# First pair's queries and keys read in fp32 by SyncE's queue and converted on chip, with the opening's order redone around it

One core of one Trainium2 chip. The metric is the device time of one execution in microseconds (us), the median of several.

## The reference

Attention with a bucketed relative-position bias, then a bilinear feed-forward layer on its output.

```python
scores = (q @ k.T) / sqrt(64) + bias_table[bucket]     # q, k, v: (8, 8, 576, 64) fp32
attn   = softmax(scores)                               # normalised after the product with v
x      = (attn @ v) -> (4608, 512)
out    = ((x @ w_a) * (x @ w_b)) @ w_out               # w_a, w_b: (512, 1536), w_out: (1536, 512)
```

## The kernel before

All work is bf16 in the matmuls. The bias enters as a product: the kernel exponentiates the bias table, writes it to DRAM as a padded table (`bias_tab`), and reads it back shifted per partition into `W`; VectorE multiplies the exponentials by `W`. Heads go in pairs (32 pairs; pairs 0 to 3 are the first batch). The first 8 pairs, "the opening", run from a hand-made list of tokens; each engine and each queue takes its own instructions in the order of the list.

```python
    def load4(src, dst, b, h0, h1):                  # GpSimd's queue: fp32 in DRAM, bf16 in SBUF
        nc.gpsimd.dma_start(out=dst[:, 256 * h0:256 * h1]..., in_=src[b, h0:h1, 0:SM, :]...)
    # ...
    nc.sync.dma_start(out=bt_sb[0:NB, :], in_=bias_table)
    nc.scalar.dma_start(out=bl_sb[0:NB, :], in_=bass.AP(...))       # last row, broadcast
    nc.sync.dma_start(out=oh_sb[0:NB, :], in_=oh_handle.ap())
    nc.scalar.dma_start(out=ident[:, :], in_=id_handle.ap())
    # ... VectorE: bt_sb - bl_sb; ScalarE: exp; TensorE: table by one-hot; VectorE: copy out
    nc.sync.dma_start(out=tab.ap(), in_=tab_sb[0:H, :])             # the table's write
    def load_w(hp, y0, y1):                                         # <W, <R: bias loads
        nc.gpsimd.dma_start(out=W_sb[hp][:, :, y0:y1], in_=bass.AP(tensor=tab, ...))
    # ...
    trb = ps_tr.tile([128, 1024], BF16, tag="tr", name="trb")       # one PSUM tile, two halves
    def tr_half(): ...                                              # in turn
```

Tokens: `<k0` a load; `TK`/`TQ`/`TZ`/`X` transposes of keys, queries, tail rows, results; `CK`/`CQ`/`CZ`/`CX` the copy out of PSUM, with `:A` for ScalarE and `:D` for VectorE; `S` scores, `E` exponential, `M` product with `W`; `T`, `ET`, `MT` the same for the tail; `AV` product with the values, `N` its normalisation; `FA`, `HA`, `FB`, `G` one bilinear unit; `w2` two filler matmuls on zeros; `P..` zero pads.

The softmax here doesn't subtract the row's maximum and nothing guards it: scores larger than these inputs give would overflow.

Of the kernel before, what the change touches and what calls it, by code (L numbers as in the profile page):

```python
# [13 lines left out]
def kernel(  # L14
# [11 lines left out]
    nc = tc.nc  # L26
    FP32 = mybir.dt.float32
    BF16 = mybir.dt.bfloat16
# [4 lines left out]
    NB = 32  # L33
    NM = 4
    SM = 128 * NM
# [3 lines left out]
    NT = B * S  # L39
# [21 lines left out]
    NR = 256  # L61
# [9 lines left out]
    assert bucket[0] == NB - 1  # L71
    oh_np = np.zeros((NB, NR), dtype=np.float32)
    oh_np[bucket, np.arange(NR)] = 1.0
    oh_handle = nc.inline_tensor(oh_np.astype(ml_dtypes.bfloat16), name="oh_const")
    id_handle = nc.inline_tensor(np.eye(128).astype(ml_dtypes.bfloat16), name="id_const")

    oh_sb = const.tile([128, NR], BF16, name="oh_sb")
    ident = const.tile([128, 128], BF16, name="ident")
    bt_sb = const.tile([128, H], FP32, name="bt_sb")
    bl_sb = const.tile([128, H], FP32, name="bl_sb")  # L80
    eb_sb = const.tile([128, H], BF16, name="eb_sb")
# [30 lines left out]
    tab_sb = wo_sb[:, :, :].rearrange("p a b -> p (a b)")[:, 0:TB]  # L112
    xn_sb = [wpool.tile([128, NT], BF16, name=f"xn{mc}") for mc in range(NMC)]
    ob_last = wpool.tile([128, DM], FP32, name="ob_last")
    g_sb = [wpool.tile([128, DM], BF16, name=f"g{df}") for df in range(NDF)]


# [99 lines left out]
    def pad_x(i, eng):  # L217
        pad(eng, XG[i][64:128, 4, :, :], 64, 128)


    nc.sync.dma_start(out=bt_sb[0:NB, :], in_=bias_table)
    nc.scalar.dma_start(out=bl_sb[0:NB, :],
                        in_=bass.AP(tensor=bias_table.tensor, offset=(NB - 1) * H,
                                    ap=[[0, NB], [1, H]]))
    nc.sync.dma_start(out=oh_sb[0:NB, :], in_=oh_handle.ap())
    nc.scalar.dma_start(out=ident[:, :], in_=id_handle.ap())
    nc.vector.memset(zero_sb[:, :], 0.0)
    nc.vector.memset(tab_sb.bitcast(FP32)[0:H, :], TWO_ONES)
    pad_ones(0)
# [79 lines left out]
    def copy(eng, out, in_):  # L309
        if eng is nc.scalar:  # L310
            nc.scalar.activation(out=out, in_=in_, func=ACTF.Copy)
        else:
            nc.vector.tensor_copy(out=out, in_=in_)
# [298 lines left out]
    def copy_x(p, jqs, eng):  # L612
        b, hp = divmod(p, 4)
        c0 = SM * B + ST * b
        ps = st[p]["tx", jqs[0]]
        q0, q1 = 128 * jqs[0], min(SM, 128 * jqs[-1] + 128)
        copy(eng, xn_sb[hp][:, SM * b + q0:SM * b + q1], ps[:, 0:q1 - q0])
        if jqs[-1] == 4:
            copy(eng, xn_sb[hp][:, c0:c0 + ST], ps[:, SM - q0:S - q0])
# [98 lines left out]
    def v_next(s):  # L718
# [7 lines left out]
    ACT = nc.scalar  # L726

    opening = """
        <k0 <q0 <k1 <q123h0 <k23 <tk <W0 <v0 <W1 <vtb <vta <tq <W2 <R0 <v1 <Wta <q123h1 <W3 <Wtb <R1
        <wa0 <k4 <wb0 <R2 <R3 <q4 <k5 <uq <q7 <q5 <wa1 <wb1 <k6 <uk <vt1b <k7 <vb1a <vb1b <vt1a <wa2 <q6  # L730
        <wb2 <wo TK0 PC0:A TQ0 PF1:D PX1:D PV1:A PU0:D CK0:A CQ00:D w1 S001 PX0:D CQ01:A S000 E001 E000
        w1 TQ30 PC1:D TK1 CK1:D TQ10 CQ10:D S011 E011 CQ30:D TK3 S100 E100 TZ1 CK3:D S301 M001 TQ20
        PV0:D TK2 E301 S101 E101 CQ20:D CK2:D w1 S200 E200 CZ1:D M000 w1 KS w1 S201 EK w2 S010 E201 V0:D
        M101 TZ0 M100 M200 M201 AV00 N00 CZ0:A AV10 E010 X00 CX00:A S300 E300 N10 T0 V1:D X10 CX10:A
        M010 ET0 AV20 TQ11 TQ21 M011 N20 CQ11:A S110 S111 CQ21:A E110 X20 M301 TQ31 M300 AV30 T1 PW:D
        MT0 AV01 CX20:D M110 E111 N30 ET1 X30 M111 CQ31:A T2 ET2 S210 CX30:D E210 PF0:A LH FA0a N01 HA0a
        MT1 TK4 X01 T3 AV11 ET3 CX01:D S211 PU1:D FB0a FA1a E211 CK4:D HA1a N11 X11 G0a M210 S310 MT2
        CX11:A E310 FB1a G1a S311 FA2a HA2a TQ4 M211 CQ4:A FB2a AV21 E311 FA3a HA3a TQ5 MT3 M310 S43 S42
        CQ5:A G2a FB3a N21 M311 TK5 E43 E42 TZ0x G3a CZ0x:D AV31 LV CK5:D N31 FA4a HA4a X21 TQ7 CQ7:A
        S41 E41 S52 E52 CX21:D FB4a FA5a HA5a X31 G4a TK6 M43 FB5a CX31:D S40 E40 S53 G5a FA0b FB0b  # L740
        CK6:D M41 TZ1x HA0b G0b CZ1x:D S51 FA1b FB1b E53 M53 HA1b G1b E51 TK7 CK7:D M40 FA2b HA2b S50
        E50 FB2b FA3b G2b HA3b V2:D T4 FB3b FA4b V3:D ET4 G3b S70 E70 M42 MT4 M52 HA4b FB4b G4b TQ6 T5
        ET5 M50 CQ6:A AV40 N40 MT5 M51 FA5b S71 E71 HA5b S73 FB5b AV41 G5b M70 N41 S72 E73 FA6f E72 T6
        M73 M71 HA6f FB6f G6f AV50 N50 S62 ET6 MT6 E62 S61 FA7f HA7f M62 AV51 N51 TH S60 E61 M61 FB7f
        G7f E60 M60 S63 E63 M63 FA8f HA8f M72 T7 FB8f G8f AV60 N60 ET7 MT7 FA9f HA9f FB9f G9f AV70 FA10f
        FB10f N70 HA10f G10f AV71 FA11f N71 FB11f X71 HA11f G11f AV61 N61 X70 FO00 FO01 FO02 HO0 CX70:D
        CX71:D
    """

    h0 = (0, 1)  # L750
# [2 lines left out]
    def step(token):  # L753
# [34 lines left out]
        if kind == "TQ":  # L788
            tr_qh(p, i[1]) if len(i) > 1 else tr_q(p)
        elif kind == "CQ":  # L790
            copy_qh(p, i[1], eng) if len(i) > 1 else copy_q(p, eng)
        elif kind == "TK":
            tr_k(p)
        elif kind == "CK":
            copy_k(p, eng)
        elif kind == "TZ":
            tr_tails(second, p)
        elif kind == "CZ":
            copy_tails(second, p, eng)
        elif kind == "KS":  # L800
            tail_keys0()
        elif kind == "EK":
            ex_keys0()
        elif kind == "S":
            qk_half(p, i[1], (i[2],)) if first else qk(p, 0, (i[1],))
        elif kind == "E":
            ex_half(p, i[1], i[2]) if first else ex(p, i[1])
        elif kind == "M":
            mul_half(p, i[1], i[2]) if first else mul(p, i[1])
        elif kind == "T":  # L810
            qk_tail(p)
        elif kind == "ET":
            ex_tail(p)
        elif kind == "MT":
            mul_tail(p)
        elif kind == "V":
            b, g = divmod(p, 2)
            v_in(b, 4 * g, 4 * g + 4, eng)
        elif kind == "AV":
            av_mm(p, jqs, *((ps_ff, "ffn") if first and i[1] == 0 and p % 2 else ()))  # L820
        elif kind == "N":
            av_norm(p, jqs)
            if 4 <= p < 7 and i[1] == 1:
                t_x(p)
        elif kind == "X":
            tr_x(p, jqs)
        elif kind == "CX":
            copy_x(p, jqs, eng)
        elif kind == "PV":
            pad_vt(0, p, eng)  # L830
        elif kind == "PC":
            pad_vt(1, p, eng)
        elif kind == "PU":
            pad_blocks(ZB[1], p, eng)
        elif kind == "PF":
            pad_blocks(tl[0], p, eng)
        elif kind == "PX":
            pad_x(p, eng)
        elif kind == "PW":
            copy(eng, Wt_sb[:, :, 0:64], Wt_sb[:, :, 64:128])  # L840
        elif kind == "LH":
            load_half(2, 0)
            load_half(2, 1)
        elif kind == "TH":
            t_half(2, 0)
        elif kind == "LV":
            load_vt(2)
        else:
            raise ValueError(token)
# [83 lines left out]
```

## Time and profile before

| | us |
|---|---|
| median of the first three runs | 414.23 (414.06 to 414.74) |
| profiled span | 412.2 |
| first scores / first exponential | 7.37 / 8.01 |
| first bias load issued / first product with it | 8.31 / 11.69 |
| first bilinear matmul | 26.55 |

The prediction shows the lines that carry its reading. One more view matters for what follows: what GpSimd's queue, on which nearly all loads are issued, waits for. In the order of time (start, length, engine, line, output and input; in brackets the idle time before it and what ended it):

```profile
8.31 0.72 POOL L252 DMA_DIRECT2D W<-bias_tab  x1 [2.66 <-DMA bias_tab<-wo]
...
28.97 0.76 POOL L270 DMA_DIRECT2D wa<-in_moe_w_a_dram  x1 [1.95 <-DMA wb<-in_moe_w_b_dram]
```

The first is the wait for the table's write. The second is a wait for the first part of `w_b`, issued at 19.39. Its landing, by the trace, was at 28.68 us (GpSimd's next issue follows 0.29 later); the first unit that reads it started at 29.43. So about 0.75 us is all the room a faster start has at that point.

### The profile page before, as it was taken

The page shows a single profiled execution, that of the slowest core. Times are in us where ns is not written, and L with a number is a line of the kernel's source. Part 1 is how long each engine was busy: PE and PEld are TensorE (multiplying, and loading weights), DVE is VectorE, ACT ScalarE, POOL GpSimd, SP SyncE. Part 2 cuts the span into 40 slices and gives each one's busy share as a digit, 9 for nine tenths or more (in the row PEclk, how much of TensorE's full clock was granted, in tenths as well). Part 3 has the DMA queues.
Part 4 walks back from the last instruction along what each step waited for, and adds up shares of the span by engine and source line. Part 5 has one row for each costly group of instructions (what it writes and reads, how often), then busy time and mean ns, then how long its engine had stood idle before and what let it go on. Part 6 is the DMA issues. An engine that isn't in the chain of part 4 may idle for free.

```text
span 412.2 us, 8768 instructions
## 1 busy us (share of the span) xinstructions
PE 404.5 (98%) x3473; PEld 210.0 (51%) x3473; DVE 240.8 (58%) x568; ACT 251.3 (61%) x384; POOL 133.6 (32%) x191
## 2 busy tenths in 40 slices
PE   8999999999999999999999999999999999999996
PEld 3576656455555455455444555555545554444443
DVE  3898997366745665476656764667547652421320
ACT  4998992676748665677556765767486642322321
POOL 6967547788029300960079004300000000000000
PEclk9999999999999999999999999999999999999999
DMA  8999999999979914995299709960520012002004
GB/s 104 179 202 189 206 166 144 160 193 142 87 133 159 139 34 91 155 129 90 41 161 143 116 16 126 127 92 17 117 67 16 17 40 78 0 9 95 2 2 102
DMA packets 135786, 42.05 MB, mean 102 GB/s; under 512 B 113688, under 2 KB 130968, under 8 KB 135744
## 3 DMA queue, kind: packets, MB, share of 16 engines
q0 software_dynamic: 81712, 20.27, 56.3%
q1 hardware_dynamic: 48592, 11.87, 18.6%
q10 hardware_dynamic: 5440, 9.34, 7.2%
q8 instruction: 27, 0.44, 0.5%
q14 instruction: 15, 0.12, 0.1%
HBM read 39.18 MB, written 9.45 MB: 118 GB/s over the span
## 4 chain that ended last, share of the span: by engine, by line
PE 94%; DVE 2%; ACT 2%; DMA 1%; issue 1%; ACTq 0%; POOL 0%; POOLq 0%
PE pb L633 23%; PE pa L633 23%; PE po L670 22%; PE av L569 8%; PE qk L406 7%; PE av L559 2%; PE av L563 2%; PE qkh L446 1%; PE qkt L479 1%; DMA qn<-in_q_dram 1%; PE trb L321 1%; ACT ath L452 1%; PE trb L415 1%; PE trb L609 0%; DVE ath L461 0%
## 5 line engine op out<-in xcount | busy, mean ns | idle before, releaser
L430 ACT ACTIVATE at<-qk 128x1024 bf16<-128x1024 f32 x112 | 113.3, 1028 | 27.5 <-DMA out_dram<-ob 10.3
L643 DVE TENSOR_TENSOR g<-pb,ha 128x512 bf16<-128x512 f32 (+1 forms) x114 | 75.6, 664 | 75.0 <-PE pb L633 58.9
L633 PE MATMUL pb<-xn,wb 128*128 128x512 bf16 (+1 forms) x456 | 112.1, 368 | 0.2 <-DVE g L643 0.2
L633 PE MATMUL pa<-xn,wa 128*128 128x512 bf16 (+1 forms) x456 | 112.1, 368 | 0.0
L640 ACT ACTIVATE ha<-pa 128x512 f32<-128x512 f32 (+1 forms) x114 | 66.2, 581 | 67.7 <-PE pa L633 66.2
L670 PE MATMUL po<-wo,g 128*128 128x512 bf16 x420 | 98.2, 379 | 0.0
L435 DVE TENSOR_TENSOR at<-at,W 128x1024 bf16<-128x1024 bf16 x112 | 75.1, 686 | 22.2 <-ACT at L430 22.1
L633 PEld LDWEIGHTS <-wa 128*128 128x128 bf16 x456 | 41.2, 98 | 46.3 <-issue 6.6
L633 PEld LDWEIGHTS <-wb 128*128 128x128 bf16 x456 | 40.6, 97 | 43.6 <-issue 5.2
L670 PEld LDWEIGHTS <-g 128*128 128x128 bf16 x420 | 38.9, 98 | 44.9 <-issue 2.5
L675 ACT ACTIVATE ob<-po 128x512 f32<-128x512 f32 x34 | 20.4, 600 | 39.9 <-PE po L670 33.6
L569 PE MATMUL av<-vm,at 128*128 128x65 bf16 x896 | 41.2, 193 | 0.0
L569 PEld LDWEIGHTS <-at 128*128 128x128 bf16 x896 | 37.4, 97 | 6.3
L132 POOL DMA_DIRECT2D qn<-in_q_dram x48 | 36.4, 807 | 12.0 <-PE qk L406 6.9
L170 POOL DMA_DIRECT2D vt<-in_v_dram x12 | 7.4, 620 | 98.9 <-PE av L563 98.1
L580 DVE RECIPROCAL rc<-av 128x6 f32<-128x6 f32 (+1 forms) x64 | 11.9, 186 | 45.2 <-PE av L569 40.8
L141 POOL DMA_DIRECT2D kn<-in_k_dram x48 | 36.2, 794 | 1.4 <-issue 0.7
L559 PE MATMUL av<-vt,att 128*128 128x130 bf16 x152 | 33.6, 221 | 0.0
L406 PE MATMUL qk<-QB,KB 64*128 64x512 bf16 x192 | 29.1, 381 | 0.0
L582 DVE TENSOR_TENSOR XG<-av,rc 128x384 bf16<-128x384 f32 (+2 forms) x64 | 27.2, 425 | 2.2
L506 ACT ACTIVATE att<-qkt 128x640 bf16<-128x640 f32 x24 | 16.8, 701 | 13.0 <-PE qkt L480 13.0
L559 PEld LDWEIGHTS <-att 128*128 128x128 bf16 x152 | 15.0, 98 | 6.5
(104 smaller groups left out, 327.0 us busy)
## 6 DMA issues: line engine op xcount, KB each, us to landing
out_dram<-ob ACTq DMA_DIRECT2D x31, 256.0 KB, 3.1
vn<-in_v_dram POOLq DMA_DIRECT2D x16, 256.0 KB, 5.8
kn<-in_k_dram POOLq DMA_DIRECT2D x48, 64.0 KB, 5.0
qn<-in_q_dram POOLq DMA_DIRECT2D x48, 64.0 KB, 4.4
wa<-in_moe_w_a_dram POOLq DMA_DIRECT2D x3, 512.0 KB, 7.4
wb<-in_moe_w_b_dram POOLq DMA_DIRECT2D x3, 512.0 KB, 9.2
wo<-in_moe_w_out_dram POOLq DMA_DIRECT2D x1, 1536.0 KB, 15.6
xn<-XG SPq DMA_TRANSPOSE x52, 3.0
```

Source lines behind the costliest of these rows:

```text
L132: nc.gpsimd.dma_start(out=by_tile(qn[b % 2])[:, h0 // 4, t, :, :], in_=q[b, h0:h1, 128 * t:128 * t + 128, :].transpose([1, 0, 2]))
L141: nc.gpsimd.dma_start(out=by_tile(kn[b % 2])[:, h0 // 4, t, :, :], in_=k[b, h0:h1, t:SM:NM, :].transpose([1, 0, 2]))
L406: nc.tensor.matmul(out=ps[:, hh, :], lhsT=kT[r, t, :], rhs=qT[r, :, :], start=True, stop=True)
L430: nc.scalar.activation(out=at[:, :, :], in_=ps[:, :, :], func=ACTF.Exp, scale=scale)
L435: nc.vector.tensor_tensor(out=at[:, :, :], in0=at[:, :, :], in1=w[:, :, S - 1 + t:S - 1 + t - SM:-1], op=MULT)
L559: nc.tensor.matmul(out=pav[:, slot, :, :], lhsT=weights_tail(p, jq), rhs=vt[i][:, :, hp, :], start=True, stop=True)
L569: nc.tensor.matmul(out=pav[:, slot, hh, :], lhsT=weights(p, t, hh, jq), rhs=vm[i][:, 2 * hp + hh, t, :], start=False, stop=True, skip_grou ...
L582: nc.vector.tensor_tensor(out=xg[:, jqs[0]:jqs[0] + m, :, :], in0=pav[:, 0:m, :, 0:Dh], in1=rc[:, 0:m, :].unsqueeze(3).to_broadcast([128, ...
L633: nc.tensor.matmul(out=ps[:, 0:n], lhsT=w[df // 4][:, mc, 128 * (df % 4):128 * (df % 4) + 128], rhs=xn_sb[mc][:, 512 * c + lo:512 * c + lo ...
L640: nc.scalar.activation(out=ha[:, 0:n], in_=ff["pa", df, lo][:, 0:n], func=ACTF.Copy)
L643: nc.vector.tensor_tensor(out=g_sb[df][:, lo:lo + n], in0=ff["pb", df, lo][:, 0:n], in1=ff["ha", df, lo][:, 0:n], op=MULT)
L670: nc.tensor.matmul(out=po[:, :], lhsT=g_sb[df][:, 128 * tt:128 * tt + 128], rhs=wo_sb[:, df, :], start=(df == 0), stop=(df == NDF - 1))
```

## The change

The intent: GpSimd's queue delivered the first pair's keys at 4.37 us (transposed from 4.70) and its queries at 6.15. SyncE's queue issues sooner (its first two loads at 0.74 and 1.21 us, GpSimd's at 1.25 and 2.06). The change leaves the casting to GpSimd's queue, which did it before; whether SyncE's could cast, no run here tries. So the two are read in fp32 into columns of `xn` that are still unused, and converted by ScalarE and VectorE. The two constants become one load, both bias inputs go to ScalarE's queue, and the whole list is ordered anew.

```diff
-    nc.sync.dma_start(out=bt_sb[0:NB, :], in_=bias_table)
+    kq32 = [xn_sb[i][:, NT - 1024:NT].bitcast(FP32) for i in range(2)]
+    def load_first(x, dst):
+        nc.sync.dma_start(out=dst.rearrange("p (h x) -> p h x", x=256),
+                          in_=x[0, 0:2, 0:SM, :].rearrange("h (p t) d -> p h (t d)", t=NM))
+    nc.sync.dma_start(out=cn_sb[:, :], in_=cn_handle.ap())       # one-hot and identity together
+    load_first(q, kq32[1])
+    load_first(k, kq32[0])
+    nc.scalar.dma_start(out=bt_sb[0:NB, :], in_=bias_table)
     nc.scalar.dma_start(out=bl_sb[0:NB, :], ...)
-    nc.sync.dma_start(out=oh_sb[0:NB, :], in_=oh_handle.ap())
-    nc.scalar.dma_start(out=ident[:, :], in_=id_handle.ap())
@@ the list: loads @@
-        <k0 <q0 <k1 <q123h0 <k23 <tk <W0 <v0 <W1 <vtb <vta <tq <W2 <R0 <v1 <Wta <q123h1 <W3 <Wtb <R1
+        <k1 <q123h0 <k23 <tk <tq <W0 <W1 <v0 <vtb <vta <W2 <q123h1 <W3 <R0 <v1 <Wta <Wtb <R1 <wa0 <k4
@@ the list: start @@
-        TK0 PC0:A TQ0 PF1:D PX1:D PV1:A PU0:D CK0:A CQ00:D w1 S001 PX0:D CQ01:A S000 E001 E000
+        PX0:A PU1:A YK0:D YQ0:A TQ0 CQ00:D CQ01:A TK0 CK0:D PU0:A PC1:D w1 S001 S000 PC0:D PV1:D E001
 [the rest of the list, all in a new order, is cut]
+        elif kind == "YK":
+            copy(eng, kn[0][:, 0:512], kq32[0])
+        elif kind == "YQ":
+            copy(eng, qn[0][:, 0:512], kq32[1])
```

More of the change, by code (lines that the diff above doesn't have):

```diff
@@ L73 @@
     oh_np[bucket, np.arange(NR)] = 1.0
-    oh_handle = nc.inline_tensor(oh_np.astype(ml_dtypes.bfloat16), name="oh_const")
-    id_handle = nc.inline_tensor(np.eye(128).astype(ml_dtypes.bfloat16), name="id_const")
-    oh_sb = const.tile([128, NR], BF16, name="oh_sb")
-    ident = const.tile([128, 128], BF16, name="ident")
+    cn_np = np.zeros((128, NR + 128), dtype=np.float32)
+    cn_np[0:NB, 0:NR] = oh_np
+    cn_np[:, NR:] = np.eye(128)
+    cn_handle = nc.inline_tensor(cn_np.astype(ml_dtypes.bfloat16), name="cn_const")
+    cn_sb = const.tile([128, NR + 128], BF16, name="cn_sb")
+    oh_sb = cn_sb[:, 0:NR]
+    ident = cn_sb[:, NR:NR + 128]
     bt_sb = const.tile([128, H], FP32, name="bt_sb")
@@ L728 @@
     opening = """
-        <k0 <q0 <k1 <q123h0 <k23 <tk <W0 <v0 <W1 <vtb <vta <tq <W2 <R0 <v1 <Wta <q123h1 <W3 <Wtb <R1
-        <wa0 <k4 <wb0 <R2 <R3 <q4 <k5 <uq <q7 <q5 <wa1 <wb1 <k6 <uk <vt1b <k7 <vb1a <vb1b <vt1a <wa2 <q6
-        <wb2 <wo TK0 PC0:A TQ0 PF1:D PX1:D PV1:A PU0:D CK0:A CQ00:D w1 S001 PX0:D CQ01:A S000 E001 E000
-        w1 TQ30 PC1:D TK1 CK1:D TQ10 CQ10:D S011 E011 CQ30:D TK3 S100 E100 TZ1 CK3:D S301 M001 TQ20
-        PV0:D TK2 E301 S101 E101 CQ20:D CK2:D w1 S200 E200 CZ1:D M000 w1 KS w1 S201 EK w2 S010 E201 V0:D
@@ L734 @@
-        M101 TZ0 M100 M200 M201 AV00 N00 CZ0:A AV10 E010 X00 CX00:A S300 E300 N10 T0 V1:D X10 CX10:A
-        M010 ET0 AV20 TQ11 TQ21 M011 N20 CQ11:A S110 S111 CQ21:A E110 X20 M301 TQ31 M300 AV30 T1 PW:D
-        MT0 AV01 CX20:D M110 E111 N30 ET1 X30 M111 CQ31:A T2 ET2 S210 CX30:D E210 PF0:A LH FA0a N01 HA0a
-        MT1 TK4 X01 T3 AV11 ET3 CX01:D S211 PU1:D FB0a FA1a E211 CK4:D HA1a N11 X11 G0a M210 S310 MT2
-        CX11:A E310 FB1a G1a S311 FA2a HA2a TQ4 M211 CQ4:A FB2a AV21 E311 FA3a HA3a TQ5 MT3 M310 S43 S42
@@ L739 @@
-        CQ5:A G2a FB3a N21 M311 TK5 E43 E42 TZ0x G3a CZ0x:D AV31 LV CK5:D N31 FA4a HA4a X21 TQ7 CQ7:A
-        S41 E41 S52 E52 CX21:D FB4a FA5a HA5a X31 G4a TK6 M43 FB5a CX31:D S40 E40 S53 G5a FA0b FB0b
-        CK6:D M41 TZ1x HA0b G0b CZ1x:D S51 FA1b FB1b E53 M53 HA1b G1b E51 TK7 CK7:D M40 FA2b HA2b S50
-        E50 FB2b FA3b G2b HA3b V2:D T4 FB3b FA4b V3:D ET4 G3b S70 E70 M42 MT4 M52 HA4b FB4b G4b TQ6 T5
-        ET5 M50 CQ6:A AV40 N40 MT5 M51 FA5b S71 E71 HA5b S73 FB5b AV41 G5b M70 N41 S72 E73 FA6f E72 T6
@@ L744 @@
-        M73 M71 HA6f FB6f G6f AV50 N50 S62 ET6 MT6 E62 S61 FA7f HA7f M62 AV51 N51 TH S60 E61 M61 FB7f
-        G7f E60 M60 S63 E63 M63 FA8f HA8f M72 T7 FB8f G8f AV60 N60 ET7 MT7 FA9f HA9f FB9f G9f AV70 FA10f
-        FB10f N70 HA10f G10f AV71 FA11f N71 FB11f X71 HA11f G11f AV61 N61 X70 FO00 FO01 FO02 HO0 CX70:D
-        CX71:D
+        <k1 <q123h0 <k23 <tk <tq <W0 <W1 <v0 <vtb <vta <W2 <q123h1 <W3 <R0 <v1 <Wta <Wtb <R1 <wa0 <k4
+        <wb0 <R2 <q4 <q5 <R3 <uq <k5 <wa1 <q7 <wb1 <uk <vt1b <vb1a <k7 <q6 <wa2 <vt1a <k6 <wb2 <vb1b <wo
@@ new lines @@
+        PX0:A PU1:A YK0:D YQ0:A TQ0 CQ00:D CQ01:A TK0 CK0:D PU0:A PC1:D w1 S001 S000 PC0:D PV1:D E001
+        E000 TK1 PV0:A CK1:D TQ10 TQ20 CQ10:D S011 E011 w1 TQ30 CQ30:D PF1:D S101 CQ20:D E101 TK2 w2 TZ1
+        CK2:D S200 M001 S100 CZ1:D E200 M000 E100 TK3 w2 KS CK3:D EK M101 TZ0 S201 E201 CZ0:D V0:D w2
+        S300 E300 M100 M201 M200 w2 S301 E301 AV10 TQ21 CQ21:A N10 PX1:D S010 E010 M300 M301 M010 T0
+        TQ11 CQ11:A ET0 AV00 T1 X10 ET1 TQ31 CX10:A N00 V1:D CQ31:A M011 PW:D MT0 S110 E110 AV30 N30 X00
@@ new lines @@
+        AV20 N20 S111 CX00:A MT1 T2 X30 E111 M111 X20 AV01 S210 CX20:A CX30:A M110 FA0a TK4 ET2 N01 T3
+        AV11 N11 E210 CK4:A HA0a X01 S211 MT2 ET3 FB0a FA1a E211 HA1a G0a X11 CX01:A S310 CX11:D E310
+        M211 S311 FB1a FA2a G1a M210 PF0:D LH M310 TQ5 TQ4 MT3 FB2a HA2a G2a CQ5:A FA3a CQ4:A AV21 N21
+        E311 M311 TZ0x TK5 FB3a S42 HA3a CK5:D CZ0x:A S43 E42 FA4a G3a HA4a AV31 LV TQ7 N31 X21 CX21:D
+        E43 S41 FB4a G4a FA5a CQ7:A X31 CX31:D S52 E41 M42 HA5a FB5a G5a FA0b TZ1x M41 E52 S40 S53 FB0b
@@ new lines @@
+        CZ1x:D HA0b G0b E40 FA1b E53 M40 V2:D TK7 FB1b S51 HA1b G1b CK7:D S50 E51 M52 FA2b HA2b FB2b G2b
+        M53 T4 FA3b M43 TK6 FB3b E50 S70 HA3b FA4b G3b CK6:D ET4 MT4 M51 E70 HA4b FB4b M50 TQ6 T5 ET5
+        G4b CQ6:A AV40 FA5b N40 S71 E71 V3:D S73 HA5b MT5 FB5b AV41 N41 E73 G5b M71 S72 E72 M72 FA6f M73
+        T6 FB6f AV50 HA6f G6f S62 ET6 E62 S61 N50 MT6 M62 FA7f HA7f AV51 N51 TH E61 M61 S60 FB7f G7f E60
+        M60 S63 E63 M63 FA8f M70 T7 FB8f HA8f G8f ET7 AV60 N60 FA9f HA9f MT7 FB9f G9f AV70 N70 FA10f
@@ L748 @@
+        FB10f AV71 HA10f FA11f G10f FB11f HA11f N71 X71 AV61 G11f N61 X70 FO00 FO01 FO02 CX71:D HO0
+        CX70:D
     """
```

## The prediction

> **What bounds the kernel now.** I read the page's first two parts, then the core view, then busy time by stretch, then the chain that ended last, then the opening instruction by instruction. Part 1 and part 2 of the page:
>
> ```profile
> PE 404.5 (98%) x3473; PEld 210.0 (51%) x3473; DVE 240.8 (58%) x568; ACT 251.3 (61%) x384; POOL 133.6 (32%) x191
> ...
> PE   8999999999999999999999999999999999999996
> ```
>
> TensorE is busy for 404.5 of 412.2 us. What any change of order can win is therefore small: 412.2 - 404.5 = 7.7 us, plus the filler matmuls on zeros that only keep the array busy. The busy-time view by stretch (busy us of each engine, then granted clock, DMA share and GB/s) says where that is:
>
> ```profile
> 0.00:5.00 5.00, 3.81 (x14) 1.09 (x16) 2.77 (x15) 2.22 (x4) 3.95 (x10) 1.00 0.54 69
> 5.00:8.00 3.00, 2.14 (x25) 1.14 (x19) 0.89 (x4) 0.98 (x2) 0.65 (x1) 1.00 1.14 143
> 8.00:14.00 6.00, 6.00 (x74) 3.17 (x70) 3.42 (x9) 4.91 (x6) 5.69 (x9) 1.00 1.20 147
> 14.00:24.00 10.00, 8.58 (x142) 5.71 (x142) 9.36 (x22) 9.66 (x15) 9.84 (x14) 1.00 1.12 182
> 24.00:60.00 36.00, 35.98 (x466) 23.92 (x463) 33.24 (x95) 32.80 (x51) 19.47 (x28) 1.00 1.45 196
> ```
>
> From 24 us to 60 us TensorE has 0.02 us to spare, and filler is absent there. From 14 to 24 us VectorE (9.36 of 10) and ScalarE (9.66 of 10) are the tight ones and TensorE has 1.42 us idle plus 1.65 us of filler (the same view for the filler's tile alone). Before 8 us all wait for data. So the opening is a start-up delay, then some 10 us paced by exponentials and table products, and then 388 us of matmuls that the change doesn't touch. The chain that ended last, in order of time (start, length, what), shows what the start-up waits for:
>
> ```profile
> 0.63 0.62 issue
> 1.25 0.81 POOL kn L123
> 2.06 4.09 DMA qn<-in_q_dram
> 6.16 0.04 issue
> 6.20 0.64 PE trb L321 x8
> 6.83 0.54 PE warm L237
> 7.37 1.02 PE qkh L446 x8
> ```
>
> The first queries are the second transfer on GpSimd's queue; they land 4.09 us after their issue, the query transposes start at 6.20 and the first scores at 7.37. The timeline has the first key transposes at 4.70, the first exponential at 8.01, and an idle ScalarE for 0.84 us before the third one at 10.79. That 6.20 is what the change attacks.
>
> [...] small loads of SyncE and ScalarE landed 1.7 to 1.9 us after their issue began, a 256 KB store of ScalarE's queue took 3.1, the first key load of GpSimd 3.45 (1.25 to 4.70). [...] the 128x512 copy in the trace took 598. [...] there are two rates, though its granted clock reads 1.00 throughout: a filler matmul lasts 0.61 us at 8.33 and 0.39 us at 13.88, four 256-column score matmuls 0.61 at 13.35 and 0.39 at 14.21. So everything TensorE does before about 13.5 us is slow, on the chain[...].
>
> **The change, part by part.**
> Removed: two casting loads at the head of GpSimd's queue, 0.82 + 0.74 = 1.56 us of its time. The next pair's keys and the other queries move up to 1.25 and 2.06, so they should land about 1.5 us sooner. The bias-table loads that follow do not gain: GpSimd idles 2.7 us for the table's write until 8.31 as it is.
> Added on SyncE's queue: one constant load (96 KB, replaces two), then queries and keys in fp32, 256 KB each. Issues there take 0.41 us, so they start at about 0.74, 1.2 and 1.6. With 1.9 us for a small load, and 1.2 more for 256 KB (3.1 - 1.9), I put the queries at 1.2 + 3.0 = 4.2 and the keys, sharing engines with GpSimd's loads, at about 4.8 (estimates).
> Added work: one ScalarE copy of 128x512 (0.60 us) and one VectorE copy (0.42 us for the 128x512 copy in the trace). ScalarE is idle enough there: its exponential of the table ends near 3.4 and the two small pads put behind it near 4.1. Queries ready at 4.2 + 0.6 = 4.8, keys at 4.8 + 0.4 = 5.2.
> Path: query transposes 4.9 to 5.5 and key transposes 5.5 to 6.1 (0.57 us each at the slow rate, now back to back), key copy on VectorE with latency to about 6.6, first scores about 6.6. Before: 7.37. Gain 0.8 us. The first exponential moves from 8.01 to about 7.2. With the next pair's data early, the 0.84 us hole before the third exponential should close: 0.8 more for ScalarE.
> Moved against it: both table inputs are now on ScalarE's queue, so the second is issued at about 1.2, not 0.74. The table exponential was held by the 1.28 us function-table load until 2.97; the input now arrives at about 3.0, plus 0.15 for the subtraction. So table write and first bias load come some 0.3 us later (8.31 to 8.6). The first table product on VectorE (11.69) can't start before that load lands: it moves to about 12.0.
> VectorE then loses 0.3 at the start, but the key and query copies that lay between its first products are already done: 0.42 + 0.42 for two copies and 0.28 for a pad before the second product at 14.40. I expect it 0.5 to 1 us ahead by 20 us. ScalarE could be 1.6 us ahead. AV products need both, so the lesser counts: 0.5 to 1 us by 24 us. Re-ordering may recover some of the 1.42 us of TensorE idle between 14 and 24: I allow 0.4. From 24 us on TensorE is full and the lead is carried to the end. Three more filler matmuls (10 for 7 in the list) cost 0.2 to 0.4 each only if they land where real work waits; I charge 0.2.
> Sum: -0.8 (middle of the lead) - 0.4 + 0.2 = -1.0, and 414.23 - 1.0 = 413.2. [...]
>
> **The rivals.**
> 1. The bias table takes over as the bound. The start-up gain is real but VectorE's products wait for the table loads, which are later by 0.3. For it: GpSimd's 2.7 us wait for the table write, and VectorE at 9.36 of 10 us. Against: VectorE had 2.58 us idle between 8 and 14 which the new order can fill with copies. Then 414.2 to 414.6.
> 2. The fp32 loads are slow: 512 KB plus 96 KB in one queue beside GpSimd's reads; the keys land at 6 instead of 4.8, and since VectorE's conversion is ahead of the query copy in its strict order, everything waits for them. For it: the median landing of GpSimd loads under load is 4 to 7 us. Against: engines are only 0.72 of 2 us busy from 2 to 4 us. First scores then at 7.8, and the time 414.3 to 415.
> 3. The whole 1.5 us lead of the early loads goes through, with an earlier end of the slow rate and the holes at 18 to 23 us closed. For it: TensorE's chain is made of slow-rate work from 6.2 to 13.4, about 7 us that would take 40% less at the fast rate. Against: ScalarE then has no room, being full from 10.8. Then 411 to 412.
>
> **Range and chances.** The three runs before spread over 0.7 us, so noise is below the effect's size. The middle case is 413.1; rivals 1 and 2 reach 415, rival 3 reaches 411. Eight times in ten between 411.5 and 414.8. Faster by over 2% would need 8.3 us, more than all idle TensorE time of 7.7 us: nearly excluded. Slower by over 2% would need the new list to open holes of 8 us; the list keeps the same work, and the order from 24 us on is nearly the same: 1%.
>
> **What would show it right or wrong.** In the changed profile: query transposes near 4.9, first scores near 6.6, first exponential near 7.2, no hole of 0.8 us between the second and third exponential, first table product near 12.0, first bilinear matmul 0.5 to 1 us before 26.55, TensorE full from there. Wrong if the transposes still start after 6; if VectorE waits for the bias load beyond 12.5; or if the first bilinear matmul gains and the end does not, which would mean a wait after 26 us that I did not see.

The sum came to 413.2. The term that took it from there to the middle case of 413.1, a shade of 0.1 us for an earlier end of the slow rate, was not shown, nor is the earlier end that rival 3 supposes. Two estimates come from the trace without saying so: a filler matmul's 0.2 to 0.4 us (spacing 0.22 us in the two at 16.31, 0.43 in the five at 1.19) and the 40% of rival 3 (eight transposes 0.57 us in the chain at 9.28, 0.34 at 27.16). GpSimd's first key load, which it puts at 3.45 us by the start of the transposes, landed in 3.1 by the trace.

## The result

416.69 us (416.59 to 417.42, six runs), the kernel before in the same rounds 414.43 (413.61 to 415.46). The ratio is 1.0058, 95% interval 1.0042 to 1.0074: 2.4 us slower, outside the predicted range of 411.5 to 414.8 and of the opposite sign. Ratios here and below are the mean time of one kernel's fast runs over that of the other's of the same rounds, so not quite the ratio of the medians quoted. A control later (e11, the same kernel once more) gave 1.0065.

The page of the changed kernel, its engine and slice lines:

```profile
PE 402.5 (97%) x3424; PEld 210.7 (51%) x3476; DVE 240.5 (58%) x566; ACT 251.6 (61%) x388; POOL 132.5 (32%) x189
...
PE   7989999999999999999999999999999999999996
```

Busy time by stretch of the changed kernel, the same columns as in the prediction:

```profile
0.00:5.00 5.00, 3.30 (x8) 0.79 (x8) 2.23 (x12) 2.48 (x5) 3.86 (x9) 1.00 0.60 140
5.00:8.00 3.00, 2.63 (x24) 1.28 (x25) 1.55 (x5) 0.94 (x3) 0.00 (x0) 1.00 1.32 174
8.00:14.00 6.00, 5.53 (x68) 2.87 (x65) 3.62 (x10) 4.20 (x6) 3.95 (x6) 1.00 0.68 84
14.00:24.00 10.00, 8.85 (x138) 5.67 (x137) 9.39 (x23) 9.98 (x14) 9.74 (x15) 1.00 1.16 185
24.00:60.00 36.00, 33.64 (x451) 23.53 (x449) 29.02 (x84) 30.00 (x51) 18.45 (x26) 1.00 1.44 196
```

Three rows differ from before. Up to 5 us the DMA engines move 140 GB/s in place of 69: the first pair now comes as fp32, and the next loads start earlier. From 8 to 14 us they move 84 GB/s in place of 147, and GpSimd issues for 3.95 us in place of 5.69. From 24 to 60 us VectorE falls from 33.24 to 29.02, ScalarE from 32.80 to 30.00 and TensorE from 35.98 to 33.64. Some matmul records are missing in this trace (3,424 matmuls for 3,476 weight loads), so TensorE's figure is too low; the control's trace, in which none are missing, has 29.75, 30.69 and 34.53. Less work got done in these 36 us. The clock column reads 1.00 everywhere; the trace has no clock record before 14.88 us here (13.86 before), and the slower rate ahead of it shows only in the length of the matmuls (two fillers 1.03 us at 12.14, 0.60 at 14.85).

Instruction by instruction, first the two lines of the kernel before that count here, then the start of the changed kernel:

```profile
8.01 1.94 ACT L452 ACTIVATE ath<-qkh 128x1024 bf16<-128x1024 f32 x2 [0.28 <-PE qkh L446]
11.69 0.69 DVE L461 TENSOR_TENSOR ath<-ath,W 128x1024 bf16<-128x1024 bf16 x1
```

```profile
4.63 0.63 ACT L320 ACTIVATE qn<-xn 128x512 bf16<-128x512 f32 x1
5.31 0.64 PE L330 MATMUL trb<-cn_sb,qn 128*64 128x128 bf16 x8
5.83 0.43 DVE L322 CAST kn<-xn 128x512 bf16<-128x512 f32 x1 [0.98 <-DMA xn<-in_k_dram]
...
7.50 1.03 PE L455 MATMUL qkh<-QT,KT 64*128 64x256 bf16 x8
...
8.14 1.94 ACT L461 ACTIVATE ath<-qkh 128x1024 bf16<-128x1024 f32 x2 [0.84 <-PE qkh L455]
...
13.14 0.69 DVE L470 TENSOR_TENSOR ath<-ath,W 128x1024 bf16<-128x1024 bf16 x1 [0.44 <-DMA W<-bias_tab]
```

The first exponential is not 0.8 us earlier but 0.13 later, and the first table product 1.45 later. The chain that ended last says why the table is late:

```profile
1.19 2.28 DMA bl_sb<-in_bias_table_dram
...
4.87 4.90 DMA bias_tab<-wo
9.77 0.28 issue
10.05 0.88 POOL W L261 x2
...
20.10 8.41 DMA kn<-in_k_dram
28.51 0.04 issue
28.55 0.41 PE trb L330 x8
```

The second bias input lands at 3.47; the table's write is issued 0.58 us later than before (4.87 against 4.29) and takes 4.9 us to land in place of 3.7 (4.29 to 8.03), so the first bias load is issued at 10.05 in place of 8.31. In this trace GpSimd's queue carries that delay to later loads, down to the keys of pair 4, for which TensorE waits until 28.55.

One trace of a start says only so much, though. The control e11 is the same kernel and lost as much time. In its trace the second input landed at 3.00, the write was issued at 4.40 and the first product ran at 12.62; the first bias load came at 9.18:

```profile
9.18 1.45 POOL L261 DMA_DIRECT2D W<-bias_tab  x2 [4.28 <-DMA bias_tab<-wo]
```

That is 0.87 us later than before, not 1.74, and TensorE waits for no keys there. Of the eleven traces with these loads and the second input second on ScalarE's queue, seven issue the write at 4.39 to 4.47 and four at 4.86 to 5.06. So the slow write shows in both traces of the changed kernel (4.9 and 4.5 us to land), the late input and the wait for keys in one only, and the loss is there without these two. What TensorE waited for from 14 to 60 us (total, times, longest), changed kernel:

```profile
PE trb L330 <- DMA kn<-in_k_dram: 0.8, 1, 0.8
PE av L578 <- DVE vm L322: 0.7, 1, 0.7
PE qkt L494 <- ACT att L523: 0.5, 1, 0.5
PE qk L415 <- ACT at L439: 0.4, 1, 0.4
PE trb L618 <- ACT QT L320: 0.3, 1, 0.3
PE warm L246 <- issue: 0.2, 1, 0.2
```

and in the kernel before:

```profile
PE qkh L446 <- ACT QT L311: 0.6, 1, 0.6
PE trb L609 <- DVE XG L582: 0.5, 1, 0.5
```

From this I took two theories. T: the bias table's path is the new bound. L: the new list costs by itself. More came later.

### The profile page after: what moved, and what is told of

It is laid out like the page before. It is cut to its first block, busy times and chain, and to the rows that moved or that the text cites. A ratio compares the mean times of both kernels' runs of the same rounds, so it can differ in the third digit from the quotient of the medians.

```text
span 415.3 us, 8728 instructions
## 1 busy us (share of the span) xinstructions
PE 402.5 (97%) x3424; PEld 210.7 (51%) x3476; DVE 240.5 (58%) x566; ACT 251.6 (61%) x388; POOL 132.5 (32%) x189
## 4 chain that ended last, share of the span: by engine, by line
PE 87%; DMA 4%; POOL 2%; ACT 2%; issue 2%; DVE 2%; ACTq 0%; DVEq 0%
PE pb L642 22%; PE pa L642 22%; PE po L679 22%; PE qk L415 7%; PE av L578 7%; PE av L568 2%; DMA kn<-in_k_dram 2%; PE av L572 2%; PE qkt L488 1%; DMA bias_tab<-wo 1%; POOL W L261 1%; PE trb L424 1%; DMA bl_sb<-in_bias_table_dram 1%; ACT att L523 0%; DVE ath L470 0%
## 5 line engine op out<-in xcount | busy, mean ns | idle before, releaser
L642 PE MATMUL pa<-xn,wa 128*128 128x512 bf16 (+1 forms) x439 | 110.6, 368 | 0.7
L679 PE MATMUL po<-wo,g 128*128 128x512 bf16 x403 | 95.5, 379 | 0.8
```

What stands on the lines that cost most here:

```text
L642: nc.tensor.matmul(out=ps[:, 0:n], lhsT=w[df // 4][:, mc, 128 * (df % 4):128 * (df % 4) + 128], rhs=xn_sb[mc][:, 512 * c + lo:512 * c + lo ...
L679: nc.tensor.matmul(out=po[:, :], lhsT=g_sb[df][:, 128 * tt:128 * tt + 128], rhs=wo_sb[:, df, :], start=(df == 0), stop=(df == NDF - 1))
```

## The experiments

All ratios are to the kernel before in the same rounds. 1% is 4.1 us. Where two runs are compared by their ratios, the errors of both count: for two intervals of 0.15% to each side, about 0.2%.

| run | what | median us | ratio (95% interval) |
|---|---|---|---|
| e1 | bias inputs side by side again | 417.27 | 1.0080 (1.0064 to 1.0095) |
| e2 | tail loads behind the bias loads | 416.97 | 1.0082 (1.0065 to 1.0100) |
| e3 | new loads, old list | 414.89 | 1.0023 (1.0010 to 1.0036) |
| e4 | old loads, new list | 415.59 | 1.0040 (1.0027 to 1.0053) |
| e5 | one copy back to VectorE | 415.86 | 1.0055 (1.0035 to 1.0074) |
| e6 | and one exponential earlier | 416.56 | 1.0068 (1.0047 to 1.0089) |
| e7 | e4 with both | 414.55 | 1.0025 (1.0003 to 1.0048) |
| e8 | keys behind the bias loads | 417.73 | 1.0099 (1.0079 to 1.0119) |
| e9 | list cut, old loads (four fast) | 420.35 | 1.0151 (1.0132 to 1.0170) |
| e10 | list cut, new loads (four runs) | 422.26 | 1.0205 (1.0186 to 1.0224) |
| e11 | the changed kernel again | 416.49 | 1.0065 (1.0049 to 1.0081) |
| e12 | nothing beside the table | 420.18 | one run |
| e13 | e9, old order of loads | 416.74 | 1.0062 (1.0046 to 1.0078) |
| e14 | e10, old order of loads | 416.70 | 1.0063 (1.0047 to 1.0079) |
| e15 | kernel before, queries first | 413.54 | 0.9982 (0.9967 to 0.9997) |
| e16 | list and loads cut, old loads | 413.47 | 1.0005 (0.9976 to 1.0035) |
| e17 | list and loads cut, new loads | 414.82 | 1.0033 (1.0011 to 1.0056) |
| e18 | kernel before, two more fillers | 413.85 | 0.9999 (0.9983 to 1.0016) |

### The table's inputs, and what is ahead of its write: e1, e2, e8, e12

```diff
 e1, SyncE's queue:   + bt_sb   cn_sb   q   k          (bt_sb no more on ScalarE's)
 e2, GpSimd's queue:  - <k1 <q123h0 <k23 <tk <tq <W0 <W1
                      + <k1 <q123h0 <k23 <W0 <W1 <tk <tq
 e8:                  + <k1 <q123h0 <W0 <W1 <k23 <tk <tq
 e12:                 + <W0 <k1 <q123h0 <k23 <tk <tq <W1
```

> The changed kernel with one move: the bias table's first load goes back to the head of SyncE's queue, so the two table inputs are issued side by side at 0.74 us. Theory T (the bias table's path is the new bound: inputs 0.98 us later, its write 0.58 us later and then stuck 4.9 us in the queues, bias loads 1.74 us later): the table product starts near 3.0 instead of 3.57, the table's write is issued near 4.3, the first bias load near 9.3 to 9.5 instead of 10.05, and the time falls from 416.7 by 0.5 to 1 us, to about 416. Theory L (the new order of the opening costs by itself): the first bias load may move, the time stays at 416.7 within 0.3.

> The changed kernel with the two loads of the tail rows (1,024 packets of 128 bytes) behind the first two bias loads on GpSimd's queue instead of ahead of them. Theory T with the part that the table's write (8 packets) is held up by packets that other queues have put on the same engines before it: its packets move before 7.5 us (7.94 to 9.22 in the changed kernel), the first bias load is issued near 8.5 instead of 10.05, the time falls by 1 to 2 us, to 415 or 415.5. If the write is slow of itself or behind SyncE's own loads, the first bias load stays near 10 and the time near 416.7. Theory L: 416.7 whatever the bias load does.

> The changed kernel with the keys of pairs 3 and 4 (512 packets) and the tails behind the first two bias loads on GpSimd's queue. Theory Q (the table's write, on SyncE's queue, moves only after what all queues have given the same engines before it: 1,152 packets of 512 bytes were ahead of it, 768 in the kernel before, and taking only the 128-byte tail packets away did not help since it left the 1,152): the write's packets move before 7 us, the first bias load is issued at 7.5 to 8.3 instead of 10.05. The time need not fall as much, since the later keys and tails now land near 13: 415 to 417. If the write is slow for another reason, the first bias load stays at 9.5 to 10.

> A measurement, not a candidate: the changed kernel with the first bias load at the head of GpSimd's queue, so that GpSimd sends nothing until the table's write has landed and SyncE's fp32 loads and the table's write have the engines to themselves. Theory Q: the keys land within 3.2 us of their issue at 1.73 (conversion on VectorE by 5.0 instead of 5.83), and the table's write lands 2 to 2.5 us after its issue instead of 4.9. If instead both are slow of themselves, the conversion stays at 5.7 or later and the write takes over 4 us. The time gets worse by 2 us or more in either case, since all other loads come late.

e1: the write was issued at 4.28, as forecast, and the first bias load at 9.57, but the fp32 queries, now one place later on SyncE's queue, were converted only at 6.15 and the first exponential came at 9.59. No time was won (1.0080). Against the control's 9.18 the bias load did not even come sooner, so e1 says little on theory T. e2: the first bias load stayed at 9.90. The forecast for the tail packets missed, and the outcome noted for a write that is slow of itself or behind SyncE's own loads came; e8 and e12 show that it was something else. e8: the first bias load moved to 7.06, and the time was still 417.73. The line that shows it:

```profile
7.06 1.45 POOL L261 DMA_DIRECT2D W<-bias_tab  x2 [4.30 <-DMA bias_tab<-wo]
```

The product that needs it started at 13.92 all the same, since VectorE's order puts the third pair's key copy ahead of it and those keys now came late. e12, with GpSimd silent until the table was there:

```profile
6.65 0.83 POOL L261 DMA_DIRECT2D W<-bias_tab  x1 [6.21 <-DMA bias_tab<-wo]
```

The write took 1.5 us to land (4.87 to 6.35, the bias load's issue following at 6.65) and the keys were converted at 4.95 in place of 5.83. So both are slow in the changed kernel because of what else is in flight, not of themselves. The packets in the kept traces say how: the write's 8 packets started at 5.65 to 5.89 us with nothing of GpSimd's ahead; at 5.78 to 6.21 in e8 with 640 packets of 512 bytes issued before it; in e2, with 1,152 issued before it, seven at 7.39 to 7.88 and the last at 9.18; at 7.94 to 9.22 in the changed kernel, with the 1,152 and the first tail load's packets. When the first of the 8 started, 519 of the 640 had started in e8, 1,006 of the 1,152 in e2 and 1,105 in the changed kernel. So the write moved behind most of what GpSimd's queue had been given before it, nearly in the order of issue over both queues. SyncE's own fp32 loads, ahead of it on its queue, are not the reason in e2 and the changed kernel: their last packets ended at 5.37 and 5.49. In e8 they ended at 5.86, so there they may be. Taking the casting loads of the first pair away did not empty the road: it moved the next 1,152 packets ahead of the table, beside 608 KB of SyncE's.

So theory T is half right: the table is late because its write is. But no run hastened the table alone. e1 puts the fp32 pair one place back and e8 the later keys, and each then waits for what it has put back.

### Loads against list: e3, e4, and the control e11

e3 has the changed kernel's loads and the list of before (conversions first, `TQ0` ahead of `TK0`); e4 the reverse.

> The fp32 loads of SyncE, the merged constants and the table inputs on ScalarE's queue as in the changed kernel, but the opening list of the kernel before (both conversions put ahead of it, queries transposed before keys, only one tail load ahead of the bias loads). Theory T: the table is late here too (inputs at 3.5, write near 4.9), but with half the tail packets ahead of it; first bias load near 9 to 9.5, time 415 to 416. Theory L: nearly all of the loss is gone, 414.0 to 414.6.

> The new opening list with all loads as in the kernel before: queries and keys cast by GpSimd's queue at its head (queries first), bias inputs side by side, separate constants. Theory T: the table's write is issued near 4.3 and lands near 8.5 to 9 (both tail loads are still ahead of it), time 414.3 to 415.5. Theory L: the loss stays, 416.3 to 417.

> The changed kernel itself once more, as the control on the chip of these runs: ratio 1.005 to 1.007.

The shares add up: 0.23% for the loads (1.0 us) and 0.40% for the list (1.7 us), 2.6 us together, against 2.4 and 2.7 us for the whole change in its two measurements. Neither T nor L alone was right. In e3 the first exponential came at 9.06, 1.05 us later than before, and the end was 1.0 us later. That the two are alike may be chance: at the first bilinear unit e3 was 0.60 late.

For the list the traces say where. Between the first weight load of the first bilinear unit and the first weight load of `FA5b`, the last 256-column unit of `w_a`, lies the same TensorE work in all kernels (the tokens are the same, but for their order):

| kernel (list in this stretch) | first unit, us | `FA5b`, us | between |
|---|---|---|---|
| before (old) | 26.55 | 50.25 | 23.70 |
| e3 (old) | 27.15 | 51.27 | 24.12 |
| changed (new) | 27.16 | 53.70 | 26.54 |
| control e11 (new) | 26.88 | 52.63 | 25.75 |
| e4 (new) | 25.66 | 51.45 | 25.79 |

With casting loads the new list was 0.9 us ahead at the first unit and 1.2 behind at the last. It loses 2.1 us after 26 us, in the part that I had called nearly the same. The changed kernel's 26.54 holds the wait of 0.8 for pair 4's keys, which the control's 25.75 has not. And e15 and e18, with the old list, take 23.77 and 24.21, so the old list's advantage is 1.5 to 2.1 us. Part of the lead at the first unit is work put off: the new list has two exponentials (`ET2`, `E210`) behind `FA0a` that the old one has ahead of it.

### Why the second part of the new list is slow: e5, e6, e7

ScalarE sat idle 2.14 us before a copy of tail queries, and 1.42 us before a tail exponential. Changed kernel, ScalarE's and VectorE's timeline:

```profile
38.76 0.77 ACT L320 ACTIVATE ZB<-trb 64x256 bf16<-64x256 bf16 x2 [2.14 <-DVE KT L322]
...
51.05 0.28 ACT L522 ACTIVATE att<-trb 128x128 bf16<-128x128 f32 x1 [1.42 <-PE pa L642]
```

```profile
38.30 0.43 DVE L322 COPY KT<-trb 128x512 bf16<-128x512 bf16 x1
...
50.54 0.41 DVE L322 COPY KT<-trb 128x512 bf16<-128x512 bf16 x1
```

Each starts within 0.1 us of the end of a VectorE copy out of the other half of the same PSUM tile, `trb`, the shared bank of what follows (38.73 and 50.95), and the trace's semaphores show that ScalarE waits for VectorE there, though no data pass between the two (for the second the view names TensorE, the last to come). So ScalarE took its turn after VectorE, idle for 2.14 us before two copies that took 0.77; what put the wait into the program the trace does not show.

```diff
 e5:  - CK5:D CZ0x:A      + CK5:D CZ0x:D
 e6:  e5, and  - ... CK6:D ET4 MT4     + T4 FA3b M43 ET4 TK6 ... CK6:D MT4
 e7:  e4 with both
```

> The changed kernel with one word changed: the copy of the second batch's query tails out of the shared transpose bank goes from ScalarE back to VectorE. Theory R (two engines that read the same PSUM tile are made to take turns, and the new list puts such turns where the partner is far behind: ScalarE sat idle 2.14 us before this copy, until VectorE's key copy out of the other half of that bank had ended): ScalarE's hole at 36.6 to 38.8 us is gone, the two holes of TensorE at 40.3 (0.34) and 42.0 (0.31) go with it, the time falls by 0.6 to 1.2 us from 416.7 to 417. Theory W (ScalarE waited because VectorE's work was late, not because of the turn): the hole moves to the next instruction and the time stays within 0.3 us.

> The changed kernel with the tail copy on VectorE and also the fifth pair's tail exponential taken ahead of the sixth key copy out of the same bank (before it waited 1.42 us for that copy, and TensorE 0.48 us for the exponential). Theory R: the hole of TensorE at 51.8 goes as well, the time is 1.3 to 2.1 us below the changed kernel, 414.7 to 415.5, what is left against the kernel before is the loads' share, about 1 us as with the old list. Theory W: 416.3 or more.

> The new list with the loads of the kernel before and the same two repairs. That list with old loads was 0.9 us ahead of the kernel before at the first bilinear matmul and 1.2 behind at the end of the opening. Theory R: most of those 2.1 us come back, the time is 413.0 to 414.0, at or below the kernel before (413.9 to 414.4). Theory W: 415.3 to 415.8 as without the repairs.

In e5's trace ScalarE's hole of 2.14 us is gone, and so is TensorE's wait of 0.4 us for a ScalarE exponential. But two other holes of ScalarE, of as much in sum, stand in its place, one of them again behind a VectorE copy out of `trb`:

```profile
36.94 1.03 ACT L439 ACTIVATE at<-qk 128x1024 bf16<-128x1024 f32 x1 [1.07 <-PE qk L415]
...
40.22 0.60 ACT L320 ACTIVATE QT<-trb 128x512 bf16<-128x512 bf16 x1 [1.06 <-DVE xn L322]
```

The hole moved, as theory W said. The stretch is 25.34 us, 0.4 less than the control's 25.75 (the changed kernel's 26.54 is no measure, for its wait for keys), and the timed gain by ratios (1.0055 against 1.0058 and 1.0065) is 0.1 to 0.4 us, within the intervals: unclear. e6 removed the second wait and made another. Its trace:

```profile
49.31 0.60 PE L642 MATMUL pa<-xn,wa 128*128 128x256 bf16 x4 [0.80 <-ACT ha L649]
```

The exponential taken ahead holds up the copy that frees a bilinear bank. 1.0068: the forecast of 1.3 to 2.1 us missed. e7 gained 0.6 us over e4 (1.0040 to 1.0025, intervals that overlap) and did not reach the kernel before. So turns on the shared bank are shown in the traces as holes of ScalarE, which move when their cause goes. That they cost time is not shown: e5's and e7's gains lie within the errors, and e6 has none.

### Which half of the list: e9, e10, e13, e14, e16, e17

The list was cut at the first bilinear unit: new order before it, old order after it. Three tries.

```diff
 e9, e10:   new order of all loads           (e9 casting loads, e10 fp32 loads)
 e13, e14:  old order of all loads
 e16, e17:  loads cut too: new order up to <wb0, old order of the rest
```

> A cut through the list: the new order up to the first bilinear matmul, the order of the kernel before from there on, with the loads of the kernel before. Theory P (the new list is good in its first half, where it was 0.9 us ahead at the first bilinear matmul, and bad in its second, where it lost 2.1 us by turns on shared banks): no hole of TensorE over 0.3 us after 26 us, still 0.5 to 0.9 us ahead of the kernel before at the end of the opening, ratio 0.998 to 0.9985 (0.6 to 0.9 us faster than before). Theory S (the lead of the first half is only work put off, which costs later in any order): holes appear in the second half as well, ratio 1.000 to 1.004.

> The same cut list with the changed kernel's loads (fp32 pair on SyncE's queue, one constant load, bias inputs on ScalarE's queue). Theory P: what is left against the kernel before is the loads' share, 1.0 us by the run with the old list, less the 0.9 of the first half: ratio 0.9995 to 1.002, that is 1.5 to 2 us below the changed kernel. Theory S: within 0.5 us of the changed kernel.

> The cut list again (new order of the computing instructions up to the first bilinear matmul, old order after it), now with every load, and the order of all loads on GpSimd's queue, as in the kernel before (queries of the first pair ahead of its keys). In the first try the old second half met the new order of loads, and TensorE waited 4.9 us for keys that the new order loads later. Theory P (the first half of the new list is worth 0.9 us, its second half loses 2.1): ratio 0.9975 to 0.999. Theory S (the lead is only put off work): 0.9995 to 1.003.

> The same with the fp32 pair on SyncE's queue and the bias inputs on ScalarE's. Theory P with the loads costing about 1 us against casting loads: ratio 0.9995 to 1.002, 2 us below the changed kernel. Theory S: 1.003 or more.

> The cut list with the loads cut as well: new order of loads and of computing instructions for the first half, old order of both for the second, casting loads as in the kernel before. Both earlier tries were spoilt by a half of one list meeting the other's loads (4.9 us wait for keys, 2.5 us wait for queries). Theory P (first half of the new list worth 0.9 us, second half costs 2.1): no wait of TensorE over 0.6 us after 14 us, ratio 0.997 to 0.999. Theory S (the lead is only put off work, lost again in any second half): 0.9995 to 1.003.

> The same cut with the fp32 pair on SyncE's queue and the bias inputs on ScalarE's. Theory P: 1 us above the run with casting loads, ratio 0.9995 to 1.0015, so 2 us below the changed kernel (1.0058 to 1.0065). Theory S: 1.003 or more.

The first two tries failed for a reason of their own, seen in e10 and in e13 (all waits of TensorE in e13):

```profile
45.74 0.64 PE L330 MATMUL trb<-cn_sb,kn 128*64 128x128 bf16 x8 [4.91 <-DMA kn<-in_k_dram]
```

```profile
PE trb L330 <- DMA qn<-in_q_dram: 3.5, 2, 2.4
```

The new list loads the keys of pair 6 later than the old second half wants them, and the old list loads the second queries later than the new first half wants them. Such holes are 4.9 us long in e10, 2.4 in e13 and 2.0 in e14. In e10 and e13 the granted clock is lower near them: half rate from 45.18 to 52.00 us in e10 (0.66 on average from 44 to 54), 0.84 on average from 14 to 24 in e13, where it was 0.72 from 8 to 14 already; which of the two brings the other is not shown. One execution of e9, the profiled one, had a mean granted clock of 0.568 and took 668.5 us; it is not used.

e16 and e17 are free of such holes (TensorE's longest waits after 14 us are 0.7 and 0.8): 1.0005 against e4's 1.0040, and 1.0033 against the control's 1.0065. The old second half, with the old order of its loads, gives back 0.32% to 0.35%, 1.3 to 1.4 us, with either kind of loads. Each of the two differences lies only just outside its error of about 0.3%, and against the first measurement of the change (1.0058) e17 wins 0.25%, within it; that both kinds of loads agree is the support. How much of it is the order of loads and how much that of the instructions is not separated. The new first half is worth nothing that can be measured: e16's interval spans 1 (four of its runs at 413.1 to 413.6, two at 415.0 and 416.8). The forecast of a gain of 0.4 to 1.2 us was not borne out; both runs lie in the ranges given for the rival S, that the lead of the first half is only work put off. In their traces the first bilinear unit came at 27.29 and 27.25, no longer ahead.

e17 over e16 prices the loads once more: 0.28%, 1.2 us. Of the other pairs that differ in the loads alone, e10 over e9 gives 0.54%, e6 over e7 0.43%, e14 over e13 0.01%. e9, e10, e13 and e14 hold the holes above, so they are weak evidence, but the loads' price is known only as 0 to 0.5%, with 0.23% and 0.28% from the pairs with the fewest holes.

### What a lead at the start is worth: e15, e18

```diff
 e15:  - <k0 <q0 ... TK0 PC0:A TQ0 PF1:D PX1:D PV1:A PU0:D CK0:A CQ00:D w1 S001 PX0:D CQ01:A S000
       + <q0 <k0 ... PC0:A PV1:A TQ0 CQ00:D CQ01:A TK0 CK0:D PF1:D PX1:D PU0:D w1 S001 PX0:D S000
 e18:  - TK0 PC0:A TQ0           + TK0 w2 PC0:A TQ0
```

> The kernel before with only the start turned round: queries of the first pair loaded and transposed ahead of its keys, both key and query copies early on VectorE, nothing else. With the new list and casting loads this brought the first exponential from 8.00 to 6.94. Theory B (after the start, VectorE's table products and so the bias loads bound the opening): first exponential near 7, first table product still near 11.7, and the time within 0.3 us of before. Theory E (the exponentials bound it): the lead of 1 us is carried, ratio 0.9975 to 0.9985.

> The kernel before with two filler matmuls in the 0.9 us gap between the first key and the first query transposes, nothing else. The full rate of TensorE was granted from anywhere between 4.4 and 20.3 us in the traces so far (13.86 before, 14.88 and 14.40 in the changed kernel), so single traces compare starts at different rates. Theory C (the moment of the full rate is worth time, and denser filler brings it forward): full rate from before 11 us, ratio 0.997 to 0.9985. Theory N (it is worth nothing, ScalarE and VectorE pace that stretch): ratio 0.999 to 1.001 wherever the full rate begins.

In e18's trace TensorE's full rate was granted at 6.02 us (key transposes 0.64 us at 4.70, query transposes 0.41 at 6.16), and at 13.86 in that of the kernel before; that the two fillers did it, one trace does not show. The first exponential came at 7.52 and the first bilinear unit 0.62 us before that of the kernel before. At `FA5b` 0.10 us was left of it, and the time is the same (0.9999). This line says where the lead went:

```profile
29.36 0.61 PE L633 MATMUL pb<-xn,wb 128*128 128x256 bf16 x4 [0.41 <-DMA wb<-in_moe_w_b_dram]
```

TensorE came early and waited for the weights, which come when GpSimd's queue brings them (landed at 29.31 here). In e15's trace (full rate from 16.35; key transposes still 0.64 us at 5.82) the first exponential was at 7.66 and the first bilinear unit 0.08 us ahead. Its time of 413.54, ratio 0.9982, beats both kernels by a little, 0.7 us with an interval of 0.1 to 1.4. The ratio lies in the range of theory E, but the first exponential was 0.35 us ahead and not 1, and the interval reaches into the range of B: undecided. The trace does not show where the gain is: at `FA5b` it is 0.01 us ahead. Of these kernels it is the one to keep, though another round could take the gain away.

## Why the prediction was wrong

Two steps failed. The lead at the start never came, since the keys landed 4.1 us after their issue and not 3.2 and the table's write took 4.9 us and not 3.7. And what comes after 24 us, taken as unchanged and full, was changed by the new list and cost 1.3 to 1.4 us.

**"I put the queries at ... 4.2 ... and the keys ... at about 4.8"**: the queries landed at 4.26, as worked out, and the keys at 5.80; VectorE had waited 0.98 us for them. The mis-sized term is the keys' landing: 4.1 us from issue in place of 3.2. e12 measures 3.2 us without GpSimd's traffic, so the estimate is right for an empty road and the contention was left out. The casting pair of the kernel before landed 3.1 and 4.1 us after issue, the fp32 pair the same, so only an earlier issue was won, and the conversions came on top. From there the path ran as drawn (conversion 5.83, key transposes 6.31, key copy 7.01): first scores came at 7.50, not 6.6, and the gain of 0.8 us became a loss of 0.13. This is rival 2 almost as written (keys at 6, first scores at 7.8). The prediction set it aside by a misread column: "only 0.72 of 2 us busy" is a share, 0.72 of the 16 engines' time from 2 to 4 us, and from 4 to 6 us it was 1.11 (packets overlap).

**"So table write and first bias load come some 0.3 us later"**: they came 0.58 and 1.74 later in the first trace, 0.11 and 0.87 in the control's. So the inputs' delay was about right on the whole (2.28 us for the second input in one trace, 1.80 in the other, where 1.8 was assumed). What was left out is the write: 4.9 and 4.5 us to land in place of 3.7, behind loads that had moved up. I had counted the earlier issue of those loads as a gain alone. This is rival 1, with the first bias load three to six times later than I sized it. But the table is not the one bound either: e8 hastened it by 2 to 3 us and won nothing, because what it put behind the table was then waited for.

**"From 24 us on TensorE is full and the lead is carried to the end"**: the changed kernel had no lead to carry, but where there was one it was not carried. Most of e18's, and all of e4's, was gone 4 to 25 us later. The wait at the weights by which e18 lost 0.41 us does not show in the profile before, since TensorE came there 0.75 us after they had landed. A wait that is nearly met looks like no wait.

**"388 us of matmuls that the change doesn't touch" and "the order from 24 us on is nearly the same"**: this is the step that failed by most. I compared the sets of tokens done by certain marks and found them alike; within them the order of loads, the engine of four copies (`CK4`, `CX01`, `CX11`, `CZ0x`) and the turn on the transpose bank had changed. By e16 and e17 this part costs 1.3 to 1.4 us.

**Right in part**: the next pair's keys landed 1.7 us sooner (5.50 for 7.24; 1.5 was forecast). The hole of ScalarE between its second and third exponentials closed (8.14 + 1.94 = 10.08, third at 10.28, 0.84 us of idle before), but nothing was won by it: holes of 0.40 and 1.26 us opened before the fourth and fifth, and at 13.97 ScalarE starts its fifth exponential where before it had started its sixth at 13.99. Conversions cost what was worked out (0.63 and 0.43 us against 0.60 and 0.42); the change stays within 2%.

In sum: loads about 1.0 to 1.2 us slower (0 to 0.5% over all pairs), second part of the list 1.3 to 1.4, first part 0 within its error of 1.2. Open stay the parts within the 1.3 to 1.4: the order of the loads, the bank turns and the exponentials put off are candidates, and e5 to e7 don't price the turns. Also, a single trace of a start compares little by itself: the full rate was granted anywhere from 4.4 to 20.3 us in these traces.

## What to carry to other kernels

Before moving a load to another queue, count what then stands ahead of the transfer on which the next stage hangs, over all queues, and in what order: here the table's write landed in 1.5 us with nothing of GpSimd's ahead (e12) and in 4.9 with 1,152 packets of 512 bytes and a tail load's ahead. A lead at the start counts only up to the first load or bank that was nearly late before (0.62 us at the first bilinear unit in e18, 0.10 left at `FA5b` after the wait for `w_b`), so look for waits that are met with little to spare. When an order is redone, compare for each engine what it must wait for, above all turns on a shared PSUM bank (2.14 us of idle ScalarE), and don't mix halves of two orders without their loads (4.9 us of idle TensorE in e10).

## What these runs show of the queues and the clock

- The write's 8 packets on SyncE's queue did not pass GpSimd's backlog soon. They moved at 5.78 to 6.21 us with 640 packets ahead (e8) and mostly at 7.39 to 7.88 with 1,152 ahead (e2), the first of them when 1,006 of these had started: nearly in order of issue. Those packets of GpSimd's are of 512 bytes, the write's of 2,176; the trace does not name the engine that moves a packet.
- From issue to landing SyncE's two loads of 256 KB in fp32 took 3.1 and 4.1 us beside GpSimd's loads (the second 3.2 without them, e12), and GpSimd's two casting loads in the kernel before 3.1 and 4.1: no gain, and the conversion (0.63 and 0.43 us) comes on top.
- The first full-rate moment of TensorE spread from 4.4 to 20.3 us over the traces of this family (13.86 before, 14.88 and 14.40 in the changed kernel and its control). In e18's trace the grant came 7.8 us earlier than in that of the kernel before, and the time differs by 0.01% (interval 0.17% to each side; the grants of the untraced executions are not known).
- One execution of e9 on a single core had a mean granted clock of 0.568 and took 668.5 us, its others, at 0.992 to 0.995, 419.4 to 420.6. Why, no run here shows.
- A turn on a shared PSUM tile with a partner far behind in its own order: ScalarE was idle for 2.14 us before two copies that took 0.77, until VectorE's copy out of the other half had ended.
